# Attention and mixture of experts in one kernel: batch 0's last expert worked as a slot

## The chip, the cores and the metric

The kernel runs on one core of a Trainium2 chip. The metric is the device time in microseconds of one execution. The two kernels are timed beside each other, and an execution of each is profiled.

## What is computed

The reference is clustered attention followed by a dense mixture of experts. Attention (4 batches, 8 heads, 768 tokens, 64 values a head) lets a query see the keys of its own cluster only; its result, as x of 3072 tokens by 512, goes through all eight experts, and every expert's output is weighted by a gate that eight rounds of row and column normalisation make:

```python
x = attn(q, k, v, centroids)                  # 3072 x 512, batch after batch
P = exp(x @ w_gate - max)                     # 3072 x 8
for _ in range(8):
    P /= P.sum(1, keepdims=True) + 1e-09
    P /= P.sum(0, keepdims=True) + 1e-09
    P *= N / E
for e in range(8):
    out += P[:, e:e+1] * (maximum(x @ w1[e], 0) @ w2[e])   # 512 -> 1024 -> 512
```

## The kernel before, in words

**Stages.** The program has an attention stage, then batch 0 of the mixture of experts (lines 1422 to 1676), then batches 1 to 3 (from line 1678). Every matmul is three fp16 matmuls (high by high, high by low, low by high parts), since the reference is fp32. Scales that are powers of two (`s1`, `s2` for an expert's two matrices, `so`, `sx`) keep the parts in range. They come from the largest absolute value of a matrix.

**Seven products for eight.** Layer 1 (`layer1`, `product`, L1356) cuts 512 x 1024 weights and 512 x 768 inputs into quadrants and takes seven products of sums of quadrants, so that one step is seven products of six matmuls with 384 columns. A step treats a quarter (`f2`, 256 columns) of an expert's first matrix. The seven quadrants or sums of the weights are `A22, A11, A12, S1, S2, S3, S4`; each is stored with its high and low part in DRAM, in `w1d[i]` for step i of 32 and in `w2d[e]` for the second matrix of expert e.

**Batch 0** runs 32 steps t = 0..31, four an expert. Within a step there are seven sub-steps m = 0..6. Each emits one product of layer 1, and from m = 1 on it emits also a piece of six matmuls with 512 columns of the layer 2 of the step before (`layer2`, L1540 to L1542): layer 2 takes the eight-product form in this stage, 144 matmuls an expert. Beside these, generators are advanced a bit per sub-step: `making` turns the raw fp32 weights of step t+1 into parts (ScalarE scales and rounds, GpSimd sums and subtracts, VectorE makes the second matrix's low part), `scanning` finds the largest values of weights on ScalarE (`total`, L302) and sends them through DRAM to all partitions (`spread_powers`), `inputs` makes the inputs of batch 1, and in steps 1 to 5 the rounds of the gate normalisation ride on spare PSUM columns (`sink`). In m = 1 `store_w` (L1525) stores the finished weights for the later batches. Raw weights come in tiles of 1 MB, two loads of 512 KB each (`load_raw`, L1438), 8 tiles deep; raw tile t+7 is loaded in step t and scanned in step i-5. In the last step the four quarters of expert 0's second matrix get their sums (`second_left`, L1501), since expert 0's second matrix had been made early, and the inputs of batch 1 are loaded again (`reload_x`). At the end of an expert, `gated` (L1547) adds the gated output of six PSUM banks to `acc` by VectorE (ScalarE copies for expert 0, and `gate_first`, L1561, scales these in step 6); for expert 7 ScalarE's queue sends `acc` out. Behind the last step stands its layer 2 alone.

**Batches 1 to 3** are a list of 24 slots (batch, expert). A slot is 28 sub-steps; each emits one product of layer 1 of slot n (`layer1b`) and a quarter of one product of layer 2 of slot n-1 (`layer2b`, L1814: nine matmuls with 256 columns). Layer 2 takes seven products too, 252 matmuls an expert. What else is to be done in a slot is a table of times written out by hand (`at`, `plan_slot`, L1741): GpSimd's differences of quadrants (`minus`, L1699), the high parts `ho` on ScalarE (`high`, L1704), the low parts on VectorE (`low`, L1708), loads of the weights (`load_left`, L1712), the gates (`gate_slot`, L1736) and, during batch 1, the sums of the second matrix of experts 1 to 7 (`second_sums` and its kin). `HASTE` (L1739) replaces some of these times in the last slot. `evict` (L1781) adds a product to the four totals `C11, C12, C21, C22`. The first slot has no layer 2 beside it, and behind the last slot stands a layer 2 alone.

**Order.** After each sub-step `plan.keep_order()` pins the order of the instructions on each engine, the DMA issues on SP's queue among them, as the program emits them. A waiting instruction holds up what is behind it on its engine.

## Time and profile before

| | |
|---|---|
| time, median of 3 runs | 2287.81 us (2287.72 to 2290.61) |
| the profiled execution: time | 2289.5 us |
| the profiled execution: span from first to last instruction | 2287.7 us |
| mean granted TensorE clock | 0.998 |
| TensorE busy | 2257.7 us, 99% of the span |
| VectorE busy | 1637.3 us, 72% |
| ScalarE busy | 1113.2 us, 49% |
| GpSimd busy | 1145.9 us, 50% |
| weights' loads (TensorE), busy | 1523.3 us, 67% |
| DMA | 383.93 MB, mean 168 GB/s |

PE is the matmul side of TensorE, PEld its weight loads, DVE is VectorE, ACT ScalarE, POOL GpSimd, SP the engine whose queue issues nearly all DMAs (SPq, ACTq: instructions that issue DMAs on a queue). Times are us from the start of the span. A matmul's busy time overlaps the next one's, so the length of a stretch is read from the starts. A bracket behind a row of a timeline is the idle time of the engine ahead of the instruction and what ended it.

### The profile page before, as it was taken

The numbers are of one execution on the slowest core, as the hardware profiler recorded it, in microseconds if no ns is written. First come the engines' busy times: TensorE is split into PE (matmuls) and PEld (weight loads), VectorE is DVE, ScalarE is ACT, GpSimd is POOL, SyncE is SP. The second block draws the span as 40 slices with busy tenths as digits, with TensorE's granted clock in tenths as the row PEclk, the third lists the DMA queues.
The fourth block names the chain that finished last, engine by engine and source line by source line (L and its number), as shares of the span: only waits on it lengthen the run. The fifth ranks groups of instructions, "written<-read, shape, count | busy, mean of one in ns | idle before, by whom it ended". The sixth has DMA issues, their size and how long they took to land.

```text
span 2287.7 us, 39676 instructions
## 1 busy us (share of the span) xinstructions
PE 2257.7 (99%) x15491; PEld 1523.3 (67%) x15491; DVE 1637.3 (72%) x2691; ACT 1113.2 (49%) x2048; POOL 1145.9 (50%) x1009
## 2 busy tenths in 40 slices
PE   7999999999999999999999999999999999999998
PEld 4656665545555555567777777777777777777777
DVE  7767777648666776578888886776676666666667
ACT  5666676556666665344444443333434333333333
POOL 6676777865554555456566563333332323222233
PEclk9999999999999999999999999999999999999999
DMA  7556666446645643676666665544444554344433
GB/s 173 120 125 162 168 157 159 118 167 239 196 150 170 195 158 131 221 262 212 211 233 219 226 222 177 169 128 152 151 159 137 187 169 133 129 132 137 143 116 102
DMA packets 226828, 383.93 MB, mean 168 GB/s; under 512 B 73408, under 2 KB 154640, under 8 KB 226128
## 3 DMA queue, kind: packets, MB, share of 16 engines
q1 hardware_dynamic: 226208, 379.82, 52.6%
q8 instruction: 121, 1.98, 0.4%
q10 hardware_dynamic: 432, 1.57, 0.2%
q14 instruction: 67, 0.55, 0.1%
HBM read 272.22 MB, written 80.62 MB: 154 GB/s over the span
## 4 chain that ended last, share of the span: by engine, by line
PE 92%; DVE 3%; DMA 2%; ACT 1%; POOL 1%; issue 1%; SPq 0%; ACTq 0%; DVEq 0%; POOLq 0%
PE h_ps L1356 37%; PE pb L1814 12%; PE pc L1814 8%; PE pa L1814 8%; PE av_ps L978 5%; PE o_ps L1540 3%; PE o_ps L1542 3%; PE o_ps L1541 3%; PE max_ps L835 3%; PE exp_ps L923 3%; PE exp_ps L924 2%; PE misc_ps L636 1%; PE misc_ps L1020 1%; POOL psum L945 1%; DVE mrt L839 1%
## 5 line engine op out<-in xcount | busy, mean ns | idle before, releaser
L1356 PEld LDWEIGHTS <-wa 128*128 128x128 f16 x5376 | 525.7, 98 | 300.0 <-issue 2.1
L1814 PEld LDWEIGHTS <-ho 128*128 128x128 f16 x6048 | 591.4, 98 | 139.7 <-DVE ho L1708 2.5
L1356 PE MATMUL h_ps<-xsT,wa 128*128 128x384 f16 x3072 | 581.6, 326 | 0.3 <-DVE u L1370 0.2
L1699 POOL TENSOR_TENSOR B<-B,B 128x768 f32<-128x768 f32 x96 | 196.5, 2049 | 488.2 <-DVE ho L1708 468.0
L1356 PE MATMUL h_ps<-xsB,wa 128*128 128x384 f16 x2304 | 436.7, 326 | 0.3 <-ACT m L1379 0.3
L1708 DVE TENSOR_TENSOR ho<-B,ho 128x768 f16<-128x768 f32 x288 | 350.2, 1217 | 0.1
L1370 DVE SCALAR_TENSOR_TENSOR u<-h_ps,m 128x384 f32<-128x384 f32 x256 | 141.7, 554 | 271.1 <-PE h_ps L1356 267.0
L1854 ACT ACTIVATE B<-B 128x384 f32<-128x384 f32 x288 | 149.7, 520 | 378.8 <-DVE B L1370 375.4
L1814 PE MATMUL pb<-w2o,ho 128*128 128x256 f16 x2592 | 328.7, 273 | 0.4 <-DVE ho L1708 0.4
L1704 ACT CAST ho<-B 128x768 f16<-128x768 f32 x288 | 230.3, 825 | 11.2 <-POOL B L1699 7.8
L839 DVE TENSOR_REDUCE mrt<-max_ps 128x1 f32<-128x512 f32 (+1 forms) x288 | 190.5, 685 | 54.3 <-PE max_ps L835 52.7
L945 POOL TENSOR_TENSOR psum<-psum,pe 128x512 f32<-128x512 f32 x160 | 208.0, 1318 | 35.0 <-ACT pe L930 28.1
L1814 PE MATMUL pa<-w2o,ho 128*128 128x256 f16 x1728 | 219.2, 273 | 1.2 <-DVE ho L1708 1.2
L1814 PE MATMUL pc<-w2o,ho 128*128 128x256 f16 x1728 | 219.2, 273 | 0.2 <-DVE ho L1708 0.2
L1699 POOL TENSOR_TENSOR B<-B,T 128x768 f32<-128x768 f32 x48 | 94.6, 1973 | 230.0 <-DVE ho L1708 207.7
L930 ACT ACTIVATE pe<-exp_ps 128x512 f32<-128x512 f32 x288 | 166.9, 598 | 51.2 <-PE exp_ps L924 39.5
L1379 ACT ACTIVATE m<-h_ps 128x384 f32<-128x384 f32 x128 | 62.6, 489 | 191.0 <-PE h_ps L1356 187.2
L1852 ACT ACTIVATE B<-h_ps 128x384 f32<-128x384 f32 x96 | 47.1, 490 | 203.3 <-PE h_ps L1356 203.3
L1542 PE MATMUL o_ps<-wb,hl 128*128 128x512 f16 x384 | 145.5, 379 | 0.0
L1541 PE MATMUL o_ps<-wb,hh 128*128 128x512 f16 x384 | 145.5, 379 | 0.0
L1540 PE MATMUL o_ps<-wb,hh 128*128 128x512 f16 x384 | 145.5, 379 | 0.0
L1370 DVE SCALAR_TENSOR_TENSOR B<-h_ps,u 128x384 f32<-128x384 f32 x192 | 105.9, 552 | 48.3 <-PE h_ps L1356 48.2
(266 smaller groups left out, 3320.8 us busy)
## 6 DMA issues: line engine op xcount, KB each, us to landing
wa<-w1d SPq DMA_DIRECT2D x98, 896.0 KB
w2o<-w2d SPq DMA_DIRECT2D x168, 512.0 KB
raw<-in_moe_w SPq DMA_DIRECT2D x64, 512.0 KB
w1d<-wa SPq DMA_DIRECT2D x30, 896.0 KB
r<-in_moe_w SPq DMA_DIRECT2D x28, 512.0 KB
w2d<-w2s SPq DMA_DIRECT2D x28, 512.0 KB
w2d<-wb SPq DMA_DIRECT2D x96, 128.0 KB
scan<-in_moe_w SPq DMA_DIRECT2D x32, 256.0 KB
```

The source lines that it names most:

```text
L839: nc.vector.tensor_reduce(out=t["mr"][:, i0 : i0 + ni, ni - 1], in_=ps.rearrange("p (x c) -> p x c", x=ni), axis=AX, op=ALU.max)
L930: nc.scalar.activation(pe, ps.rearrange("p (x c) -> p x c", x=ni), AF.Exp, scale=SCALE)
L945: (nc.gpsimd if e == POOL else nc.vector).tensor_tensor(out=st[:, o : o + N0], in0=old[o], in1=part, op=ALU.add)
L1356: nc.tensor.matmul(ps[:, 0:HB], wa[:, w_, a, c, :], x[:, x_, c, :], start=(first and s_ == 0), stop=(s_ == len(steps) - 1), skip_group_che ...
L1370: nc.vector.scalar_tensor_tensor(out=t, in0=ps[:, 0:HB], scalar=KAPPA, in1=x, op0=ALU.mult, op1=ALU.add)
L1540: nc.tensor.matmul(po[i], hh[:, t, ti], wbh[:, t], start=(first and t == 0), stop=False)
L1541: nc.tensor.matmul(po[i], hh[:, t, ti], wbl[:, t], start=False, stop=False)
L1542: nc.tensor.matmul(po[i], hl[:, t, ti], wbh[:, t], start=False, stop=(last and t == 1))
L1699: nc.gpsimd.tensor_tensor(out=t, in0=d[a], in1=d[c], op=ALU.subtract)
L1704: nc.scalar.copy(t[:, 0], blocks[n, g][o])
L1708: nc.vector.tensor_tensor(out=t[:, 1], in0=blocks[n, g][o], in1=t[:, 0], op=ALU.subtract)
L1814: nc.tensor.matmul(ps[:, q], h[:, h_, f, q * P : (q + 1) * P], w[:, 2 * g + f, w_], start=(first and g == 0 and s_ == 0 and q % 2 == 0), s ...
```

## The change

Batch 0 now has 28 steps (`N1`), for experts 0 to 6. Expert 7 of batch 0 becomes the first entry of the list of slots, so there are 25 slots and its second matrix takes seven products as well. `acc` is no longer one tile but the four totals `C11, C12, C21, C22`, in which the slot goes on adding; an eviction in batch 0 becomes two operations of half the width, and batch 0's output leaves by the slots' four stores on SP. Expert 7's weights are made by a new generator, `lasting`, which starts at step 1 and is advanced in every sub-step: it loads both matrices in eight tiles of 512 KB (two deep) for the sums of absolute values, sends the largest through DRAM, then loads them once more, quarter by quarter, and makes and stores all seven quadrants or sums of both matrices. Expert 0's left-over sums (`second_left`, `step_left`) go; in their place expert 0 takes part in batch 1's `second_sums`, and expert 7 no longer does. The raw tiles are 7 instead of 8, loaded six steps ahead instead of seven. The inputs of batch 1 are reloaded in the last quarter of the first slot. In the last slot four entries of `HASTE` change or are new, and the gates are made ten sub-steps earlier.

The diff, cut to its core:

```diff
-        rawp = pool("rawp", 8, ax)
-        accp = pool("accp", 1, ax)
+        rawp = pool("rawp", 7, ax)
+        lastp = pool("lastp", 2, ax)
+    N1 = NI - NP2
+    PARTS = {"C11": (0, 0), "C22": (1, 1), "C12": (0, 1), "C21": (1, 0)}
+    accb = pool("accb", 1)
...
+        def last_first(f2):
+            raw, w = load_last(0, f2), last_tile()
...
+            yield
+            yield
+            nc.scalar.activation(raw, raw, AF.Copy, scale=s1[:, E - 1 : E])
+            yield
...
+            for o, a in quads:
+                nc.scalar.copy(y[:, 0, o], a)
+            yield
+            for o, a in quads:
+                nc.gpsimd.tensor_tensor(out=y[:, 1, o], in0=a, in1=y[:, 0, o], op=ALU.subtract)
+            yield
+            yield
+            nc.sync.dma_start(out=d[:, :, A22 : A12 + 1], in_=y)
...
+            sums(S_, A[:, 1, 0], A[:, 1, 1], A[:, 0, 0], A[:, 0, 1], nc.gpsimd)
...
+            nc.scalar.copy(y[:, 0], S_)
+            yield
+            for o in (0, 2):
+                nc.gpsimd.tensor_tensor(out=y[:, 1, o : o + 2], in0=S_[:, o : o + 2], in1=y[:, 0, o : o + 2], op=ALU.subtract)
+                yield
+            yield
+            nc.sync.dma_start(out=d[:, :, S1 : S4 + 1], in_=y)
...
+        def last_second(f2):
...
+            for o, a in quads:
+                nc.scalar.activation(y[:, o, 0], a, AF.Copy, scale=scale)
+            yield
+            for o, a in quads:
+                nc.vector.scalar_tensor_tensor(out=y[:, o, 1], in0=a, scalar=scale, in1=y[:, o, 0], op0=ALU.mult, op1=ALU.subtract)
...
+        def last_weights():
+            am = gs.tile([P, 2, NP2], F32, name="am8z", bufs=1)
+            waiting = []
+            for f2 in range(NP2):
+                for m in range(2):
+                    waiting.append((m, f2, load_last(m, f2)))
+                    yield
+                    if len(waiting) == 2:
+                        m_, f_, t = waiting.pop(0)
+                        total(am[:, m_, f_ : f_ + 1], t, t)
+                    yield
+            m_, f_, t = waiting.pop(0)
+            total(am[:, m_, f_ : f_ + 1], t, t)
+            yield
+            am2 = gs.tile([P, 2], F32, name="am2")
+            nc.vector.tensor_reduce(out=am2, in_=am, axis=AX, op=ALU.max)
+            yield from spread_powers(am2, 2, f"amw{E - 1}", lambda g: weight_use(E - 1, g, gs))
+            for f2 in range(NP2):
+                yield from last_first(f2)
+                yield from last_second(f2)
...
-                if e == 0:
-                    nc.scalar.copy(acc[:, i], ps)
-                else:
-                    gate = gates_[:, i : i + 1]
-                    nc.vector.scalar_tensor_tensor(out=acc[:, i], in0=ps, scalar=gate, in1=acc[:, i], op0=ALU.mult, op1=ALU.add)
-                if e == E - 1 and i % 2 == 1:
-                    nc.scalar.dma_start(out=out_v[0][:, i - 1 : i + 1], in_=acc[:, i - 1 : i + 1])
+                j, q_ = divmod(i, NT // 2)
+                for name, (r, j_) in PARTS.items():
+                    if j_ == j:
+                        t, s_ = acc[name][:, q_], ps[:, r * HD : (r + 1) * HD]
+                        if e == 0:
+                            nc.scalar.copy(t, s_)
+                        else:
+                            nc.vector.scalar_tensor_tensor(out=t, in0=s_, scalar=gates_[:, i : i + 1], in1=t, op0=ALU.mult, op1=ALU.add)
...
-        AHEAD = 7
+        AHEAD = 6
...
-        loads = {0: (), 1: (4, 5), 2: (6, 7, 8), 3: (9, 10)}
+        loads = {0: (), 1: (4, 5), 2: (6, 7, 8), 3: (9,)}
-        for t in range(NI):
+        for t in range(N1):
...
+            if t == 1:
+                lasting = last_weights()
...
                 if m:
                     step(before)
-                if t == NI - 1:
-                    step_left(m)
+                step(lasting)
                 if m == 1:
                     store_w(t, wt)
-                if t == NI - 1:
-                    reload_x(1, RIGHT[m])
...
-    slots = [(b, e) for b in range(1, B) for e in range(E)]
+    slots = [(0, E - 1)] + [(b, e) for b in range(1, B) for e in range(E)]
...
-    HASTE = {("T1", 1): (3, 3), ("T2", 0): (2, 4), ("T2", 1): (4, 5)}
+    HASTE = {("T1", 1): (3, 3), ("T2", 0): (1, 2), ("T2", 1): (4, 5), ("B21", 0): (5, 7), ("B21", 1): (6, 8)}
...
-        at(base - 1, gate_slot, n)
-        if e == E - 1:
+        at(base - (11 if n == NS - 1 else 1), gate_slot, n)
+        if b and e == E - 1:
...
-        if b == 1 and n:
+        if b == 1 and e < E - 1:
...
-    totals = {}
+    totals = dict(acc)
```

## Rows read from the trace of the kernel before

**Rows 1.** The page's chain that ended last: shares of the span by engine.

```profile
PE 92%; DVE 3%; DMA 2%; ACT 1%; POOL 1%; issue 1%; SPq 0%; ACTq 0%; DVEq 0%; POOLq 0%
```

**Rows 2.** Windows: us, busy us (instructions), clock, DMA share, GB/s; an expert, a slot.

```profile
735.69:794.07 58.38, 58.38 (x314) 30.53 (x313) 41.70 (x63) 38.19 (x63) 32.10 (x33) 1.00 0.57 185
1052.90:1107.70 54.80, 54.80 (x423) 41.09 (x421) 47.21 (x66) 24.14 (x39) 37.29 (x27) 1.00 0.60 182
```

**Rows 3.** Chain in time order: start us, us, what; first products of batch 0 steps.

```profile
532.06 1.95 PE h_ps L1356 x12
...
546.93 1.97 PE h_ps L1356 x12
...
722.98 1.95 PE h_ps L1356 x12
...
941.90 1.95 PE h_ps L1356 x12
```

**Rows 4.** Timeline, PE: layer 2 of the first and of the last slot begins.

```profile
993.00 1.15 PE L1814 MATMUL pa<-w2o,ho 128*128 128x256 f16 x9
...
998.16 1.14 PE L1356 MATMUL h_ps<-xsT,wa 128*128 128x384 f16 x6
...
2252.91 4.09 PE L1814 MATMUL pa<-w2o,ho 128*128 128x256 f16 x36
```

**Rows 5.** Timeline, PE: the second and third product of the first slot.

```profile
965.08 1.14 PE L1356 MATMUL h_ps<-xsT,wa 128*128 128x384 f16 x6
...
966.49 1.14 PE L1356 MATMUL h_ps<-xsB,wa 128*128 128x384 f16 x6 [0.28 <-ACT m L1379]
```

**Rows 6.** Timeline, PE: layer 2 alone, the last phase.

```profile
2256.84 2.35 PE L1814 MATMUL pc<-w2o,ho 128*128 128x256 f16 x20
...
2267.13 3.88 PE L1814 MATMUL pa<-w2o,ho 128*128 128x256 f16 x34 [1.16 <-DVE ho L1708]
...
2270.85 4.09 PE L1814 MATMUL pb<-w2o,ho 128*128 128x256 f16 x36
```

**Rows 7.** Timeline, DVE: the last phase.

```profile
2252.96 1.31 DVE L1411 TENSOR_SCALAR gates<-pr,so 128x6 f32<-128x6 f32 x1
...
2264.95 1.25 DVE L1789 SCALAR_TENSOR_TENSOR C<-pc,gates,C 128x256 f32<-128x256 f32 x3
```

**Rows 8.** Windows, columns as in rows 2: batch 0's first steps.

```profile
495.00:500.00 5.00, 5.00 (x46) 2.62 (x44) 2.67 (x7) 1.01 (x2) 0.00 (x0) 1.00 0.67 275
500.00:505.00 5.00, 5.00 (x30) 2.64 (x29) 3.99 (x10) 2.28 (x5) 0.00 (x0) 1.00 0.98 298
505.00:510.00 5.00, 5.00 (x27) 2.55 (x26) 0.98 (x3) 4.04 (x7) 3.68 (x6) 1.00 1.05 384
```

**Rows 9.** Timeline, SP's queue: step 1.

```profile
506.72 3.33 SPq L1531 DMA_DIRECT2D w2d<-wb  x3
```

**Rows 10.** Timeline, ACT: step 1.

```profile
512.99 0.53 ACT L1620 ACTIVATE hh<-c 128x384 f16<-128x384 f32 x1 [3.16 <-DVE c L1370]
```

**Rows 11.** Timeline, DVE: the end of step 3.

```profile
547.16 0.55 DVE L1370 SCALAR_TENSOR_TENSOR c<-h_ps,u 128x384 f32<-128x384 f32 x1
```

**Rows 12.** Chain in time order: an expert's largest values on their way.

```profile
701.34 5.63 DMA amw<-am
...
706.98 4.81 DMA all<-amw
```

**Rows 13.** Windows, columns as in rows 2: step 6.

```profile
576.60:591.20 14.60, 14.60 (x80) 7.64 (x79) 8.46 (x17) 12.15 (x21) 7.47 (x8) 1.00 0.41 86
```

**Rows 14.** Lines by form, 500 to 955: busy us, mean ns, idle before.

```profile
L302 ACT ACTIVATE junk<-raw 128x1024 f16<-128x1024 f32 x48 | 50.1, 1045 | 0.0
...
L1564 ACT ACTIVATE acc<-acc,gates 128x512 f32<-128x512 f32 x6 | 4.3, 712 | 0.5 <-DVE gates L1411 0.5
...
L1411 DVE TENSOR_SCALAR gates<-pr,so 128x6 f32<-128x6 f32 x7 | 1.6, 222 | 0.0
...
L1494 POOL TENSOR_TENSOR wa<-s1w,wa 128x512 f16<-128x512 f32 x60 | 78.4, 1327 | 57.0 <-ACT wa L1492 53.7 <-DMA w2d<-wb 3.3
```

More of the change, by code (lines that the diff above doesn't have):

```diff
@@ L1514, in second_left @@
+            nc.scalar.activation(y[:, :, 0], S_, AF.Copy, scale=scale)
             yield
-            nc.sync.dma_start(out=w2d[0][:, 3:7, f2], in_=y)
+            nc.vector.scalar_tensor_tensor(out=y[:, :, 1], in0=S_, scalar=scale, in1=y[:, :, 0], op0=ALU.mult, op1=ALU.subtract)
             yield
-        LEFT_AT = ((0, 3, 4, 6), (1, 5, 6, 8), (2, 7, 8, 10), (3, 9, 10, 12))
-        def step_left(now):
-            for x, times in zip(lefting, LEFT_AT):
-                if now in times:
-                    step(x)
+            yield
@@ L1673, in attn_moe_kernel @@
             rests.clear()
-            step_left(7 + m)
             step(before)
@@ L1806, in layer2b @@
                 if name not in totals:
-                    totals[name] = accp.tile([P, 3, HD], F32, name=name, bufs=2 if name == "C21" else 1)
+                    totals[name] = (accx if name == "X" or (name == "C21" and b % 2) else accb).tile([P, 3, HD], F32, name=name)
             count = 0
```

85 lines of the change are left out of this document (58 added, 27 removed).

## The prediction

> **What bounds the kernel now.** I read the page's chain of waits first: TensorE holds 92% of the chain that ended last [rows 1], so what counts is where TensorE spends columns and where it stands. The windows view then gives the price of the unit that the change moves [rows 2]: over one expert of batch 0 and over one slot TensorE is busy from end to end at full clock, while VectorE, ScalarE and GpSimd have a quarter or more of the time free. The reader is to see that both are bound by TensorE, and that only their lengths differ. The chain in time order gives the length of a step of batch 0: (941.90 - 722.98) / 15 = 14.595 us, so an expert of four steps is 58.38 us [rows 3]. The timeline of TensorE gives the slot: layer 2 of the first slot begins at 993.00 and that of the last, 23 slots later, at 2252.91, so a slot is 1259.91 / 23 = 54.78 us [rows 4].
>
> **The sum, part by part.** An execution with this span of 2287.7 us took 2289.5 us (1.8 us lie around the span), 1.7 us over the median of the runs, 2287.8. I work out a difference and set it on the median.
>
> *Expert 7 becomes a slot.* One expert of 58.38 us goes, one slot of 54.78 us comes: -3.6 us. Layer 1 is the same 28 products in both; what is saved is in layer 2, 144 matmuls of 512 columns against 252 of 256. That the narrow matmuls might cost more per column is already in the slot's measured price, so this term has one answer.
>
> *The edge between batch 0 and the slots.* Today the second product of the first slot starts at 965.08 and the third at 966.49 [rows 5], 1.41 us where two products stand 0.98 us apart: 0.43 us lost, because ScalarE's queue holds the output DMAs and expert 0's left-over weights, each waiting for VectorE. Both go away. At the end of that slot two pairs and one product take 998.16 - 993.00 = 5.16 us [rows 4] where the pace of 54.78 / 28 = 1.956 us a pair gives 4.9; the 0.26 us are VectorE's, which scales `pr` there for a batch's first expert, and the new first slot has none of that. Together -0.7 us; bounds 0 and -0.9. Against this, batch 1's inputs are now reloaded during a slot in which products stand 0.98 us apart. The first, 384 KB, can be issued about 1.2 us after its product starts and is needed 6.8 us after it; a 0.9 MB weight load stands ahead, and 1.3 MB at the 384 GB/s of [rows 8] take 3.4 us. That leaves about 2 us of cover, so 0, with 2 us as the upper bound.
>
> *The last phase.* With layer 1 over, a product takes 2256.84 - 2252.91 = 3.93 us, but the next three take 2270.85 - 2256.84 = 14.01 us: 2.2 us lost, 1.16 of it in one wait for VectorE's low half of B21 [rows 4, 6]. VectorE works there without a break. The change takes the gate operation, 1.31 us long [rows 7] where its kind takes 0.22 us on average [rows 14], out of that queue to a place ten steps earlier, puts B21's low half before the three evictions that begin at 2264.95 [rows 7], and T2's before T1's second. VectorE still has the rest of its list, so I take back what leaves the list: -1.1 us, bounds 0 and -2.2. The long gate operation stands beside GpSimd work in the same stretch. The Trainium skill, "SBUF — State Buffer", section "Who interferes with whom", has VectorE and GpSimd hold a shared port pair for a whole instruction, the other blocked; by that the 1.31 us are mostly waiting, the trace agrees, and the gain would be nearer 0.2 us than 1.1 if the next VectorE instruction merely inherits the wait.
>
> *The stream that makes expert 7's weights.* It replaces work that stood in the last steps, so its amount is nearly neutral; its place is not. Four places are priced.
>
> (a) Step 1. Eight 512 KB loads now go through the SP queue in steps 1 to 3, two tiles deep. The first stands behind raw tiles 2 to 5 and ahead of the three stores issued at 506.72 [rows 9]. Batch 0's x (1.5 MB), three stores of 128 KB and four raw tiles of 1 MB are ahead of it, 5.9 MB, of which 5 us at 275 and 5 us at 298 GB/s have moved 2.9 by 505; the other 3.0 at 384 GB/s [rows 8] last until 512.9, the load until 514.3. ScalarE reaches the sum over this tile at 512.99 - 3.16 = 509.8 [rows 10]; it waits 4.5 us, of which 3.2 were idle anyway. With the sum itself (1.05 us [rows 14] and a short read behind it) it is some 2.5 us late; that reaches TensorE only through the buffers of layer 1, as 0.7 us. The bounds are 0 and 4.5. The Trainium skill, "DMA: Bandwidth & Descriptors", section "Where 436 GB/s comes from", puts HBM at about 358 GB/s a core; the row here shows 384, so the measured rate stands, and by the page's rate the wait would be 0.6 us longer.
>
> (b) Step 3. The largest of the eight sums is taken by VectorE behind the last two sums on ScalarE. Those add over 2 us to a ScalarE already some 2 us late, so VectorE stands about 2.5 us. Its cover is thin just there, since the gates' rounds ride in steps 1 to 5: the last eviction of step 3 ends at 547.71 [rows 11] and the second product of step 4, which needs that buffer, begins one product after 546.93 [rows 3], at 547.9. I take 1.5 us; bounds 0 and 4.
>
> (c) Step 3 to 4. The maximum goes to DRAM and back: the row of another expert shows 5.63 + 4.81 = 10.4 us [rows 12], and there VectorE used it after four sub-steps. The new stream uses it three sub-steps (some 6.5 us) after issue, so VectorE stands up to 3.9 us, and the sums behind it are late. TensorE needs its next result about 2.5 us later than that queue order says: 1.4 us; bounds 0 and 3.9.
>
> (d) Step 6. ScalarE is busy 12.15 of 14.60 us there [rows 13]. Scaling the totals takes twelve half-width operations for six of 0.71 us [rows 14]: with some 0.45 us each, +1.1 us; three more operations of expert 7's second matrix fall in this step, +1.3. That fills the step; 0.6 us, bounds 0 and 2.
>
> Together +4.2 us. The rest I cost at nothing, and this hides it: one step less between a raw load and its scan (7 tiles for 8) leaves 14.6 us for 1 MB, 2.7 us of transfer; if that cover goes, ScalarE waits at the head of each step. The later loads, stores and makers fall in steps where ScalarE, VectorE and GpSimd have about 5 us free of 14.6 [rows 2]. The twice as many, half as wide evictions of an expert stand on VectorE with the same 4 us a step free. Batch 0's four stores, now on SP instead of ScalarE's queue, wait for evictions as those of later batches do, with a slot of slack behind them. Expert 0's sums take the places that expert 7's had among the slots.
>
> Sum: -3.6 - 0.7 - 1.1 + 4.2 = **-1.2 us**, so 2286.6 us. A measurement of this kernel can tell about 0.2%, 4.6 us, from no change.
>
> **The rivals.**
>
> *All of it hidden.* If the stream costs TensorE nothing, -5.4 us, 2282.4 us. For it: TensorE shows almost no stall in batch 0 although ScalarE and VectorE often run late; layer 1's two buffers and the layer 2 between them absorb some 2 us. Against it: at 547.7 the slack was 0.2 us.
>
> *The early waits reach TensorE in full (slower).* In steps 1 to 4 ScalarE waits for a load and VectorE for ScalarE and then for the DRAM round trip, in order, with every eviction of layer 1 behind them. At full length 4.5 + 4.0 + 3.9 + 0.6 = 13.0 us, so -5.4 + 13.0 = +7.6, 2295.4 us. It makes the kernel slower by more than 0.2% from 10.0 us of the 13.0 on. For it: DMA runs at its highest rate there [rows 8], and VectorE's cover in step 3 is 0.2 us. Against it: each wait must first use up what layer 1's two buffers cover.
>
> *GpSimd blocks VectorE.* In steps 4 to 22 GpSimd gets some 2.3 us more a step. If in one step of three one more VectorE operation in front of TensorE stands for a GpSimd instruction of 1.33 us [rows 14], that is 6 x 1.33 = 8.0 us: 2290.4 us with the early waits hidden, 2294.6 with them. This is what the whole-instruction lock of the Trainium skill, "SBUF — State Buffer", section "Who interferes with whom", would do. Against it: VectorE has 4.2 us a step free [rows 2], and the operations that TensorE waits for read PSUM and one tile.
>
> **How the numbers follow.** The forecast, part of the early waits reaching TensorE, gets 0.54, all hidden 0.25, the early waits in full 0.13, the block by GpSimd 0.08, half of that beyond 0.2%. So faster 0.25, same 0.54 + 0.04 = 0.58, slower 0.17. The forecast's own range is 2283.5 to 2290.5. The range given reaches down to all hidden, with a little more of the last phase's 2.2 us, 2282.0, and up to 2292.2, about where slower begins, which leaves out the 0.17 and little below.
>
> **What would show it.** Right: step starts of 14.6 us from step 7 on, the first slot beginning near 910 instead of 964, 24 slot lengths of 54.8 us, the gate operation gone from the last phase and the wait of 1.16 us there shortened; in steps 1 to 4 a ScalarE wait for the load of `lw`, a VectorE wait before `am2` and for the second DRAM tile, and TensorE's steps 2 to 5 longer than 14.87 us [rows 3] by 3 to 4 us in all. Wrong: steps 1 to 5 unchanged in length (then all hidden), or steps 8 to 22 longer than 14.6 us (then GpSimd or the later loads), or a gap at the first slot's end while an input is reloaded.

## The result, and the profile after

The changed kernel takes 2310.71 us (median of 5 runs, 2307.44 to 2313.17) where the kernel before, run beside it, takes 2289.35 us (5 runs): a ratio of 1.0089, 95% interval 1.0078 to 1.0100. The change makes the kernel slower by 0.9%; the forecast was 2286.6 us. The profiled execution, the fastest of the five, took 2307.44 us with a span of 2305.6 us, 17.9 us more than the span of before; the medians lie 21.4 us apart, and the 3.5 us between the two are in no trace. The timeline of TensorE splits the 17.9 us by the starts of the same products in both kernels:

| stretch | before | after | difference |
|---|---|---|---|
| fourth product of step 0 (at 497.50) to the first of step 6 (at 576.52) | 79.02 | 88.98 | +10.0 |
| step 6 to the first slot, without one expert of 58.38 us [rows 3] | 329.20 | 340.10 | +10.9 |
| first slot to layer 2 of the last: 24 slots, then 25 | 1288.81 | 1342.93 | +54.1 |
| the removed expert | 58.38 | | -58.4 |
| last phase [rows 4, 6] | 29.91 | 31.42 | +1.5 |

The other -0.2 us lie ahead of that fourth product and behind the last matmul of layer 2. An expert as a slot with its edge is worth 54.12 - 58.38 = -4.3 us, as forecast. The loss is 20.9 us within batch 0 and 1.5 us in the last phase, and each has its place. TensorE's timeline after, of the pieces with a wait above 1 us ahead of them in batch 0 (the bracket is the wait and what ended it):

```profile
520.91 1.14 PE L1356 MATMUL h_ps<-xsT,wa 128*128 128x384 f16 x6 [2.85 <-DVE c L1370]
538.55 0.39 PE L1622 MATMUL o_ps<-wb,hh 128*128 128x512 f16 x1 [1.64 <-ACT hh L1704]
543.11 2.08 PE L1356 MATMUL h_ps<-xsB,wa 128*128 128x384 f16 x6 [2.93 <-ACT m L1379]
...
621.79 1.14 PE L1356 MATMUL h_ps<-xsB,wa 128*128 128x384 f16 x6 [2.09 <-ACT m L1379]
694.90 1.14 PE L1356 MATMUL h_ps<-xsT,wa 128*128 128x384 f16 x6 [1.69 <-DVE c L1370]
789.33 1.14 PE L1356 MATMUL h_ps<-xsT,wa 128*128 128x384 f16 x6 [2.16 <-DVE u L1370]
800.76 1.14 PE L1356 MATMUL h_ps<-xsT,wa 128*128 128x384 f16 x6 [1.22 <-DVE c L1370]
832.12 1.14 PE L1356 MATMUL h_ps<-xsT,wa 128*128 128x384 f16 x6 [1.86 <-DVE c L1370]
```

The kernel before has no wait above 0.2 us from step 7 to the end of its batch 0. The first three stand in steps 2 and 3, right behind ScalarE's waits for the first loads of expert 7 (timeline of ScalarE, after):

```profile
517.57 1.06 ACT L302 ACTIVATE lw<-lw 128x1024 f32<-128x1024 f32 x1 [7.86 <-DMA lw<-in_moe_w]
...
536.93 1.06 ACT L302 ACTIVATE lw<-lw 128x1024 f32<-128x1024 f32 x1 [5.85 <-DMA lw<-in_moe_w]
541.53 1.06 ACT L302 ACTIVATE lw<-lw 128x1024 f32<-128x1024 f32 x1 [2.62 <-DMA lw<-in_moe_w]
```

The other five lie in steps 8, 13, 19, 20 and 22. The chain of waits after, in time order (start, us, what), shows what such transfers take, the early ones and two of the later places:

```profile
506.71 10.78 DMA lw<-in_moe_w
...
531.40 10.05 DMA lw<-in_moe_w
...
595.19 5.84 DMA amw<-am
...
616.75 1.01 POOL lw L336
...
620.21 0.02 ACT lw L1577
...
783.87 8.01 DMA w1d<-wa
...
795.68 1.57 DVE wb L1476
```

At 595 it is the largest values of another expert that go to DRAM, 5.84 us for the first way; its scales come late, so do the weights of the next step, and GpSimd, late too, does expert 7's sums (`lw`, L336) only from 616.75 on, for which ScalarE stands at 620.2 with `m1` of layer 1 behind it. At 783.87 it is the store of a finished weight tile that takes 8 us, so that its buffer comes free late. The windows after (columns as in [rows 2]): four pieces of 14.6 us, the last of them step 6 [rows 13], the 5 us behind the wait at 543.11, and the ten steps 7 to 16:

```profile
504.60:519.20 14.60, 13.46 (x72) 6.75 (x69) 5.35 (x12) 5.96 (x11) 4.88 (x6) 1.00 0.99 342
519.20:533.80 14.60, 12.89 (x72) 7.12 (x73) 12.12 (x21) 10.68 (x18) 10.29 (x10) 1.00 0.89 303
533.80:548.40 14.60, 10.04 (x46) 4.78 (x45) 7.46 (x22) 8.81 (x18) 2.99 (x4) 0.88 0.97 335
586.40:601.00 14.60, 14.60 (x80) 7.63 (x79) 9.40 (x17) 12.34 (x25) 9.55 (x10) 1.00 0.60 189
543.10:548.10 5.00, 5.00 (x20) 2.60 (x20) 2.95 (x9) 4.97 (x10) 2.76 (x4) 0.66 0.91 295
...
600.97:752.30 151.33, 146.59 (x782) 76.31 (x781) 110.48 (x191) 101.35 (x173) 108.32 (x109) 1.00 0.68 219
```

In the first three DMA is nearly full (0.99, 0.89, 0.97) at 303 to 342 GB/s. The granted clock is 0.88 in the third and 0.66 behind its longest wait; these are means over time at TensorE's two levels, 1.00 (2.4 GHz) and 0.50 (1.2 GHz). In the ten steps TensorE stands for 4.7 us of 151.3 although VectorE (110.5), ScalarE (101.4) and GpSimd (108.3) all have time free.

The last phase: the timeline of TensorE after,

```profile
2269.41 4.09 PE L1894 MATMUL pa<-w2o,ho 128*128 128x256 f16 x36
...
2278.34 1.92 PE L1894 MATMUL pc<-w2o,ho 128*128 128x256 f16 x16 [2.65 <-DVE ho L1788]
...
2289.09 3.88 PE L1894 MATMUL pb<-w2o,ho 128*128 128x256 f16 x34 [0.64 <-DVE ho L1788]
```

the place of the second row in the kernel before,

```profile
2259.37 1.92 PE L1814 MATMUL pc<-w2o,ho 128*128 128x256 f16 x16 [0.18 <-DVE ho L1708]
```

and VectorE and GpSimd in the same place after:

```profile
2270.80 2.52 DVE L1788 TENSOR_TENSOR ho<-B,ho 128x768 f16<-128x768 f32 x1
2273.24 2.56 DVE L1788 TENSOR_TENSOR ho<-T,ho 128x768 f16<-128x768 f32 x1
2275.72 2.56 DVE L1788 TENSOR_TENSOR ho<-B,ho 128x768 f16<-128x768 f32 x1
...
2268.20 4.31 POOL L1779 TENSOR_TENSOR B<-B,B 128x768 f32<-128x768 f32 x2
2272.59 2.40 POOL L1779 TENSOR_TENSOR T<-B,B 128x768 f32<-128x768 f32 x1
2274.95 2.52 POOL L1779 TENSOR_TENSOR B<-B,B 128x768 f32<-128x768 f32 x1
```

The wait of 1.16 us of [rows 6] is gone, as forecast (0.64 us stand ahead of the next product instead), but T2's low half now stands ahead of T1's second, which `pc` needs. Three low halves take 2.5 us each beside GpSimd, where one alone takes 0.94 (at 2279.39), and each ends 0.8 us after one of GpSimd's instructions has ended (2272.51, 2274.99, 2277.47). TensorE waits 2.65 us for the third where it waited 0.18.

### The profile page after: what moved, and what is told of

Its sections match the earlier page's. It is cut to its first block, busy times and chain, and to the rows that moved or that the text cites. A ratio compares the mean times of both kernels' runs of the same rounds, so it can differ in the third digit from the quotient of the medians.

```text
span 2305.6 us, 40008 instructions
## 1 busy us (share of the span) xinstructions
PE 2255.9 (98%) x15599; PEld 1532.6 (66%) x15599; DVE 1662.4 (72%) x2750; ACT 1121.8 (49%) x2078; POOL 1168.2 (51%) x1017
## 4 chain that ended last, share of the span: by engine, by line
PE 87%; DMA 4%; DVE 4%; ACT 2%; POOL 1%; issue 1%; SPq 1%; DVEq 0%; ACTq 0%; POOLq 0%
PE h_ps L1356 36%; PE pb L1894 13%; PE pc L1894 8%; PE pa L1894 8%; PE av_ps L978 4%; PE max_ps L835 3%; PE exp_ps L923 2%; PE o_ps L1622 2%; PE o_ps L1623 2%; PE o_ps L1624 2%; PE exp_ps L924 2%; DMA lw<-in_moe_w 1%; PE misc_ps L636 1%; ACT pe L930 1%; PE misc_ps L1020 1%
## 5 line engine op out<-in xcount | busy, mean ns | idle before, releaser
L1894 PEld LDWEIGHTS <-ho 128*128 128x128 f16 x6300 | 616.2, 98 | 147.0 <-DVE ho L1788 4.1
L1779 POOL TENSOR_TENSOR B<-B,B 128x768 f32<-128x768 f32 x100 | 206.5, 2066 | 514.2 <-DVE ho L1788 496.5
L1788 DVE TENSOR_TENSOR ho<-B,ho 128x768 f16<-128x768 f32 x300 | 367.5, 1226 | 0.0
L1894 PE MATMUL pb<-w2o,ho 128*128 128x256 f16 x2700 | 342.5, 273 | 0.6 <-DVE ho L1788 0.6
L1784 ACT CAST ho<-B 128x768 f16<-128x768 f32 x300 | 240.0, 825 | 11.7 <-POOL B L1779 4.0
L1894 PE MATMUL pc<-w2o,ho 128*128 128x256 f16 x1800 | 228.4, 273 | 2.7 <-DVE ho L1788 2.7
L1894 PE MATMUL pa<-w2o,ho 128*128 128x256 f16 x1800 | 228.3, 273 | 0.0
L978 PE MATMUL av_ps<-pe,vn 128*64 128x512 f32 (+1 forms) x768 | 134.2, 492 | 0.0
L1622 PE MATMUL o_ps<-wb,hh 128*128 128x512 f16 x336 | 127.5, 380 | 1.6 <-ACT hh L1704 1.6
L924 PE MATMUL exp_ps<-qX,kX 98*128 98x256 f32 (+1 forms) x384 | 126.6, 342 | 1.6 <-DMA qX<-mt 1.6
```

What stands on the lines that cost most here:

```text
L924: nc.tensor.matmul(o, t["k2"][0:98, ki], t["qa"][0:98, a:z], start=False, stop=True)
L978: nc.tensor.matmul(av[o, a:z], vn[:, i, :], heads[t]["pe", c][:, i - i0], start=(i == 0), stop=False, skip_group_check=True)
L1622: nc.tensor.matmul(po[i], hh[:, t, ti], wbh[:, t], start=(first and t == 0), stop=False)
L1779: nc.gpsimd.tensor_tensor(out=t, in0=d[a], in1=d[c], op=ALU.subtract)
L1784: nc.scalar.copy(t[:, 0], blocks[n, g][o])
L1788: nc.vector.tensor_tensor(out=t[:, 1], in0=blocks[n, g][o], in1=t[:, 0], op=ALU.subtract)
```

## The experiments

Theory A: the early loss is the loads of expert 7 in steps in which DMA is full; the later one is waits in the fixed order of each queue, where the stream uses something too soon or meets other work. Theory B: the stream is too much work beside batch 0, or GpSimd, busier, blocks VectorE. Theory C: the parts of the change outside the stream. D and E are A with places named, as the results forced them.

The end of the attention stage moves by up to 5 us from run to run (the product at 497.50 of before starts between 493.6 and 498.6), so the time of one execution misleads, and stretches of the profiled execution are compared: "early" and "later" are the first two differences of the table above, against the kernel before; "slots" and "last" are the lengths. The last column is a median for before, after, e13, e15 and e16, and one execution for the others.

| kernel | early | later | slots | last | time of one execution, or median |
|---|---|---|---|---|---|
| before | 0 | 0 | 1288.8 (24) | 29.9 | 2289.35 |
| after | 10.0 | 10.9 | 1342.9 | 31.4 | 2310.71 |
| e1 start in step 5 | 0.0 | 20.2 | 1342.9 | 32.1 | 2303.95 |
| e2 old last slot | 9.4 | 12.8 | 1342.9 | 30.0 | 2304.03 |
| e3 wide | 9.5 | 2.1 | 1342.9 | 32.0 | 2300.05 |
| e4 no scan | 0.0 | 11.2 | 1342.9 | 32.2 | 2296.30 |
| e5 start in step 7 | 0.0 | 12.4 | 1342.9 | 32.1 | 2298.32 |
| e6 four things | 0.0 | 9.9 | 1346.0 | 30.3 | 2295.46 |
| e7 no way through DRAM | 11.4 | 11.8 | 1342.9 | 31.9 | 2308.63 |
| e8 late stores | 9.2 | 8.5 | 1342.9 | 32.2 | 2306.12 |
| e9 in phase | 0.0 | 8.7 | 1348.2 | 29.9 | 2298.28 |
| e10 sooner to DRAM | 8.5 | 13.2 | 1343.4 | 32.0 | 2308.52 |
| e11 e9 and e10 | 0.0 | 11.5 | 1346.9 | 29.9 | 2301.61 |
| e12 places | 0.0 | 0.9 | 1346.1 | 30.0 | 2289.79 |
| e13 parts outside the stream, in before | 0.0 | -0.3 | 1289.4 (24) | 29.9 | 2289.72 |
| e14 no GpSimd | 9.2 | 6.6 | 1342.9 | 32.2 | 2300.29 |
| e15 three tiles | 0.0 | 3.5 | 1342.9 | 30.1 | 2288.61 |
| e16 four tiles | 0.0 | 1.7 | 1342.9 | 29.9 | 2286.57 |

e2 has the changed kernel's batch 0 as it is: 9.4 and 12.8 for 10.0 and 10.9. So a difference of 2 us in one stretch of one execution says nothing.

**The early half.** e1 and e5 move the start, e4 leaves the first loads, sums and way through DRAM out, e7 the way alone.

```diff
-            if t == 1:
+            if t == 5:      # e1;  e5: t == 7
                 lasting = last_weights()
```

> The stream begins in step 5 instead of step 1; nothing else changes. Theory A (early loads of expert 7 land late because the DMA queues are full in steps 1 to 3, and ScalarE and VectorE wait for them in order): steps 1 to 4, which lost about 10 us against the kernel before, lose at most 1 us, and the kernel comes to about 2301 us; the later 11 us stay, perhaps at other steps. Theory B (the stream's work is simply too much beside batch 0, wherever it stands): the loss moves to steps 5 to 9 and the time stays at about 2310 us. Theory C (seven raw tiles or the half-width evictions are to blame): steps 1 to 4 stay as long as they are, 2310 us.

> The stream begins in step 7, when the gates' rounds, the scaling of the totals in step 6 and the way of expert 2's largest values through DRAM are over; nothing else changes. Steps 1 to 6 should be those of the kernel before. If what expert 7's sums and its way through DRAM cost in steps 7 and 8 of the start in step 5 (about 6 us) came from meeting expert 2's way through DRAM, steps 7 to 9 lose at most 1.5 us, and the batch loses about 12 us in all, by in-order waits from step 10 on. If the amount of work decides, the loss stays near 20 us.

e4, in place of the first loads and sums:

```diff
-            for f2 in range(NP2):
-                for m in range(2):
-                    waiting.append((m, f2, load_last(m, f2)))
...
-            yield from spread_powers(am2, 2, f"amw{E - 1}", lambda g: weight_use(E - 1, g, gs))
+            for _ in range(21):
+                yield
+            for t in (s1, s2, so):
+                nc.vector.tensor_copy(out=t[:, E - 1 : E], in_=t[:, 1:2])
```

> The eight first loads of expert 7, their sums on ScalarE and the way of the largest through DRAM are left out (expert 7 takes the scales of expert 1); the rest of the stream keeps its sub-steps. Theory A: steps 1 to 4 lose at most 1 us of their 10, time about 2301 us, steps 7 to 22 unchanged. If the early loss comes from the raw tiles or from the half-width evictions instead, steps 1 to 4 stay 10 us too long.

e7, with the loads and sums kept:

```diff
-            yield from spread_powers(am2, 2, f"amw{E - 1}", lambda g: weight_use(E - 1, g, gs))
+            for _ in range(4):
+                yield
+            for t in (s1, s2, so):
+                nc.vector.tensor_copy(out=t[:, E - 1 : E], in_=t[:, 1:2])
```

> The changed kernel without the way of expert 7's largest values through DRAM and without the wait for it (it takes the scales of expert 1; four sub-steps keep the rest in place). The eight loads and sums stay. If the late loads make the early loss, steps 1 to 3 lose 8 us or more as they do, and step 4 and 5 win back at most 2 us. If the way through DRAM makes it, the early loss falls below 4 us.

In e1, e4 and e5 steps 1 to 5 are those of the kernel before to 0.01 us: the eight loads with their sums make the early loss, not the raw tiles and not the evictions. Without the way through DRAM it is as large as with it (11.4), so that way costs nothing there that these runs can tell. But e1 gains nothing in sum: its loss only moves (later 20.2), 6 us of it to steps 7 and 8. There expert 2's largest values meet the stream's loads: their first way takes 8.2 us from 580.78 on, VectorE stands 3.7 us for them, and 2.1 us more for expert 7's own at 609.98. Theory A expected the 10 us back and was wrong there; B fits e1. e5, two steps later, keeps 12.4, as expected; half of this, 6.4 us, stands in step 10, where expert 7's own largest values are under way (chain of e5: start, us, what) and VectorE stands behind them in its queue:

```profile
628.69 6.42 DMA amw<-am
635.13 4.55 DMA all<-amw
```

**The last slot.** e2 takes the old places back.

```diff
-    HASTE = {("T1", 1): (3, 3), ("T2", 0): (1, 2), ("T2", 1): (4, 5), ("B21", 0): (5, 7), ("B21", 1): (6, 8)}
+    HASTE = {("T1", 1): (3, 3), ("T2", 0): (2, 4), ("T2", 1): (4, 5)}
...
-        at(base - (11 if n == NS - 1 else 1), gate_slot, n)
+        at(base - 1, gate_slot, n)
```

> The last slot's times (HASTE) and the place of the gate operation are as before the change; the rest is the changed kernel. If the reordered last slot costs what its stretch shows (three VectorE low parts in a row, each 2.5 us beside GpSimd, ahead of the third product), the last phase shrinks from 31.4 us to the 29.9 us of the kernel before, and the time by about 1.5 us. If the longer last phase comes from something else (the totals' place, the extra slot), it stays at 31.4 us.

The last phase is 30.0 us: the reordering costs 1.4 us, and up to 2.3 in the other kernels that have it. In e1 TensorE's clock falls behind the same wait, from 0.99 to 0.50, the lower of its two levels, after 2.65 us of standing. Windows of e1, columns as in [rows 2]:

```profile
2268.80:2273.90 5.10, 2.45 (x24) 1.96 (x22) 5.10 (x4) 3.14 (x5) 4.20 (x2) 0.99 0.34 103
2273.90:2277.20 3.30, 3.30 (x16) 2.38 (x17) 3.30 (x8) 0.00 (x0) 0.00 (x0) 0.50 0.00 0
```

e9, e11, e12, e15 and e16 keep only the early gates (the old `HASTE`, the gates at base - 11): 29.9 to 30.1 us, so the gate operation's absence gains nothing. Nor do B21's earlier times: e6, which keeps them with T2's old ones, has 30.3 us; the wait of 1.16 us leaves, and waits of 0.57 and 0.63 us come. VectorE's timelines tell why the gate operation is worth nothing. e2, with it:

```profile
2267.45 1.32 DVE L1411 TENSOR_SCALAR gates<-pr,so 128x6 f32<-128x6 f32 x1
...
2269.86 3.94 DVE L1788 TENSOR_TENSOR ho<-B,ho 128x768 f16<-128x768 f32 x2
```

and e16, without it:

```profile
2250.53 5.01 DVE L1815 TENSOR_TENSOR ho<-B,ho 128x768 f16<-128x768 f32 x2
```

The two low halves behind it grow from 3.94 to 5.01 us: of the 1.32 us, 1.07 are inherited. They start earlier and end at the same time, 6.39 and 6.40 us after `pa` begins (2267.41 and 2249.14), each 0.8 us behind the end of one of GpSimd's instructions (2272.99 for the second in e2, 2254.72 in e16). That is what the whole-instruction lock of the Trainium skill, "SBUF — State Buffer", section "Who interferes with whom", would do; the prediction had named it against its own term.

**What makes the later half?** e3 only widens the stream, e8 only delays its stores, e10 only starts the other experts' ways through DRAM earlier, e14 takes GpSimd's work out of it, e13 puts the parts outside it into the kernel before.

```diff
+            yield                        # e3: two more ahead of each of the four
+            yield
             nc.scalar.activation(raw, raw, AF.Copy, scale=s1[:, E - 1 : E])
...
+            yield                        # e3: one more ahead of each first store;  e8: two ahead of every store
             nc.sync.dma_start(out=d[:, :, A22 : A12 + 1], in_=y)
...
+            yield                        # e3
+            yield
             nc.scalar.copy(y[:, 0], S_)
```

> Ten sub-steps are added to each quarter of the stream: two more between a load and its first use, two more between GpSimd's sums and their rounding, one more ahead of the first store, in both matrices. The work is the same and still starts in step 1. Theory A (what is lost in steps 7 to 22 are in-order waits of ScalarE, VectorE and SP for loads, sums and low parts that are used too soon): the 11 us lost in steps 7 to 27 fall to 5 us or less, the early 10 us stay: about 2304 us. Theory B (the amount of work, or GpSimd blocking VectorE while both run): steps 7 to 27 still lose 9 us or more, 2309 us.

> Only the stream's sixteen stores come two sub-steps later (about 4 us; on SP's queue they wait 13 to 23 us a line, over 1 us each, for low parts of GpSimd and VectorE). If SP's queue, held by these waits, makes the loss of steps 7 to 22 (late stores of finished weights and late ways through DRAM of the other experts), the loss there falls from 11 to 4 us or less. If ScalarE's waits for loads and for GpSimd's sums make it, it stays at 8 us or more. The early loss stays.

```diff
                 total(ams[e][:, m, f2 : f2 + 1], raws[idx][:, m * 1024 : (m + 1) * 1024], junkp.tile([P, 1024], F16, name="junk"))
-                yield
+                if m or f2 < NP2 - 1:
+                    yield
...
         nc.sync.dma_start(out=d, in_=am)
         yield
+        if apart:
+            yield
```

> The changed kernel, with one thing changed for experts 2 to 6: both sums of an expert's last quarter stand in one sub-step, so that its largest values start for DRAM a sub-step earlier, and a sub-step more lies between the two DMAs. Theory D: the loss of steps 7 to 22 falls from 11 to 6 us or less. If the loss is in the waits for the stream's loads and GpSimd's sums instead, it stays at 9 us or more. The early loss of 10 us stays either way.

```diff
-                nc.gpsimd.tensor_tensor(out=y[:, 1, o], in0=a, in1=y[:, 0, o], op=ALU.subtract)
+                nc.gpsimd.tensor_tensor(out=y[:, 1, o, :, 0:8], in0=a[:, :, :, 0:8], in1=y[:, 0, o, :, 0:8], op=ALU.subtract)
...
-            sums(S_, r2[:, 1, 0:HD], r2[:, 0, 0:HD], r2[:, 1, HD:DO], r2[:, 0, HD:DO], nc.gpsimd)
+            sums(S_[:, :, 0:8], r2[:, 1, 0:8], r2[:, 0, 0:8], r2[:, 1, HD : HD + 8], r2[:, 0, HD : HD + 8], nc.gpsimd)
```

> The changed kernel with GpSimd's work in the stream cut to 8 columns an operation (sums and low parts are left out; the stores of the first matrix send a tile of noughts, so they wait for nobody); loads, ScalarE's and VectorE's work and all transfers stay. If GpSimd (its lock against VectorE, ScalarE's and SP's waits for its sums and low parts) makes the loss of steps 7 to 22, it falls from 11 to 4 us or less. If loads and transfers make it, it stays at 8 us or more. The early loss of 10 us stays, since GpSimd has no part in it.

```diff
-        rawp = pool("rawp", 8, ax)
+        rawp = pool("rawp", 7, ax)
...
-                    nc.vector.scalar_tensor_tensor(out=acc[:, i], in0=ps, scalar=gate, in1=acc[:, i], op0=ALU.mult, op1=ALU.add)
+                    for h in range(2):
+                        t = acc[:, i, h * HD : (h + 1) * HD]
+                        nc.vector.scalar_tensor_tensor(out=t, in0=ps[:, h * HD : (h + 1) * HD], scalar=gate, in1=t, op0=ALU.mult, op1=ALU.add)
...
-        AHEAD = 7
+        AHEAD = 6
```

> The kernel before with three of the change's parts and nothing else: 7 raw tiles, loaded six steps ahead, and evictions (and the scaling of the totals in step 6) in two halves of 256 columns. My prediction put all three at nothing. If so, the time is that of the kernel before within 1 us. If twice as many VectorE operations at an expert's end, or the later raw loads, cost something in every expert, it is 2 us or more slower.

e13 rules out Theory C: 2289.72 us (10 runs) against 2289.21, ratio 1.000, 0.999 to 1.0009; its three parts cost nothing that this can tell (2 us). e3 answers for A: the same work, and the later loss falls from 10.9 to 2.1. It also thins the work out, to 42 sub-steps a quarter of the weights where the changed kernel has 32; e16 below, with 28, shows that this is not what helps. e8 gets 2.4 back, little more than two executions of the same code differ. e10 was a miss, and so was its theory as put: 13.2 us are no fall, and beside e2's 12.8 no rise either. Its earlier start brings the largest values back no sooner. Ahead of step 15 the first way starts 2.9 us earlier, reckoned from the step's start (720.76, after 723.11), but it now stands right behind the stores of a step's weights. On SP's queue the second DMA could be issued only 9.1 us after the first (5.2 in the changed kernel at the same place), 1.1 us later than there:

```profile
709.62 1.65 SPq L1616 DMA_DIRECT2D w2d<-wb  x3
711.37 1.61 SPq L1295 DMA_DIRECT2D amw<-am  x1
720.50 0.33 SPq L1300 DMA_DIRECT2D all<-amw  x1
```

Ahead of step 19 (780.08, after 781.49) it starts 4.8 us earlier, and the second DMA leaves 1.4 us later. In both kernels a store of the stream, `w1d<-lw`, stands ahead of this DMA on SP's queue and waits for GpSimd's low part, until 780.86 in the changed kernel. SP's queue of e10:

```profile
769.34 0.35 SPq L1295 DMA_DIRECT2D amw<-am  x1
...
780.89 0.52 SPq L1537 DMA_DIRECT2D w1d<-lw  x1
781.50 0.56 SPq L1300 DMA_DIRECT2D all<-amw  x1
```

and of the changed kernel:

```profile
775.51 0.33 SPq L1295 DMA_DIRECT2D amw<-am  x1
...
780.87 0.52 SPq L1534 DMA_DIRECT2D w1d<-lw  x1
781.48 0.56 SPq L1298 DMA_DIRECT2D all<-amw  x1
```

e14 is undecided by its own bounds: 6.6, between 4 and 8. GpSimd's work takes part in some 4 us, give or take the 2 us of above, and without it TensorE still waits for VectorE, 1.73 us at 722.70 and 2.40 us at 808.64.

**Choosing the places.** e6 combines what had helped; e9, e11 and e12 place the stream by what the trace of the one before showed; e15 and e16 bring all of it back into batch 0. These five start in step 7 and give a quarter 28 sub-steps, the length of an expert.

```diff
-        if b == 1 and e < E - 1:
+        if n == 0 or (b == 1 and e < E - 1):        # e6, e9, e11, e12: expert 7's sums in the first slot
             first = base - SLOT
...
+            for _ in range(14):                     # e9, e11: between expert 7's two DMAs
+                yield
...
+            for _ in range(8):                      # and ahead of their use
+                yield
```

> Four things together: the stream begins in step 7; its way through DRAM has two sub-steps more; two sub-steps more lie between load and use and between GpSimd's sums and their rounding, and one before a store; and the sums of expert 7's second matrix move into the first slot, where the later experts' sums are made in their own slots, which makes room for the wider distances. In the last slot B21's new times and the early gates stay, T2's go back. Theory A: batch 0 loses at most 3 us against 20.9, the last phase is 28.5 to 29 us, and the time is 2284 to 2287 us, below the kernel before. Theory B: steps 9 to 27 lose 8 us or more, 2291 us or more.

> As e6 (start in step 7, sums of expert 7's second matrix in the first slot), but each quarter of the stream now takes 28 sub-steps, just as long as an expert of four steps, and is placed so that no DMA of the stream is issued in the sub-steps in which another expert's largest values go to DRAM and back (sub-steps 3 to 7 of every fourth step); expert 7's own way through DRAM has 22 sub-steps. In the last slot only the early gates stay. Theory D (what is left of the loss is VectorE waiting for these ways through DRAM, which take 5 to 8 us instead of 2.6 to 3 where the stream's transfers meet them): batch 0 loses at most 3 us against e6's 9.9, time 2283 to 2288 us. Theory B (amount of work): still 7 us or more, 2291 us or more.

> e9 and e10 together. Theory D: no loss left in batch 0 beyond 1 us, time 2282 to 2286 us. Theory B: as e9, 2291 us or more.

e6 and e9 missed by far: 9.9 and 8.7 us are left. In e6 8.9 of them lie in steps 11, 15, 19 and 23, at the four ways of other experts through DRAM, which its transfers meet. In e9 these cost nothing or little, and other meetings show. VectorE, at expert 7's own largest values:

```profile
674.28 0.77 DVE L1602 TENSOR_SCALAR gmax<-gmax 128x2 f32<-128x2 f32 x1
675.09 1.08 DVE L1603 TENSOR_SCALAR gmax<-gmax 128x2 int32<-128x2 int32 x1
676.20 1.73 DVE L270 TENSOR_SCALAR ginv<-gmax 128x2 f32<-128x2 f32 x1
```

GpSimd at the same time:

```profile
673.87 2.27 POOL L1498 TENSOR_TENSOR wa<-s1w,wa 128x512 f16<-128x512 f32 x2 [2.11 <-ACT wa L1496]
676.10 1.80 POOL L321 TENSOR_TENSOR tx<-xqB,tx 128x768 f32<-128x768 f32 x1
```

Operations of 0.17 us in the kernel before take 0.77, 1.08 and 1.73 us here, each ending within 0.03 us of one of GpSimd's (675.03, 676.14, 677.90), and TensorE waits 1.27 and 1.24 us behind them. And where expert 7's low parts on VectorE meet the evictions of the expert before, e9 loses 1.2 to 1.4 us each time. e11 adds e10's step to e9 and loses 2.8 us more, all in steps 15, 19 and 23, those of the other experts' ways. e12 moves just these places (the diff is cut; its third place is in the first slot):

```diff
-                yield from last_first(f2)
-                yield from last_second(f2)
+                yield from last_second(f2)
+                yield from last_first(f2)
...
-            for _ in range(8):                     # from e9's way back to the use of its largest values
+            for _ in range(5):
```

> As e9 (start in step 7, sums of expert 7's second matrix in the first slot, quarters of 28 sub-steps), with three places moved that e9's trace shows late: the second matrix' low parts on VectorE go from the sub-step in which the evictions of the expert before begin to one without them; the use of expert 7's own largest values goes five sub-steps ahead, away from GpSimd's differences for batch 1's inputs; and in the first slot the four sums stand further from their rounding. Theory E (what is left, 8.7 us in batch 0 and some 2.6 us in the first slot, comes from the places where the stream's VectorE and GpSimd work meets other work): batch 0 loses 4 us or less, the first slot nothing, time 2285 to 2290 us. Theory B (the amount of work): batch 0 still loses 7 us or more.

The later loss falls to 0.9 us, with e9's work and its two tiles of 512 KB. What keeps it from gaining is the first slot, 3.2 us longer: there a product takes 0.98 us, the four sums' loads and stores crowd the transfers, and batch 1's inputs are late:

```profile
937.22 1.14 PE L1356 MATMUL h_ps<-xsB,wa 128*128 128x384 f16 x6 [2.10 <-DMA xsB<-xsd1B]
```

So e15 and e16 keep every sum in batch 0, with the two matrices' work side by side in three and four tiles of 512 KB:

```diff
-        lastp = pool("lastp", 2, ax)
+        lastp = pool("lastp", 4, ax)               # e15: 3
...
+            for i in range(29):                    # each operation of a quarter at a sub-step written out by hand
+                for time, f in todo:
+                    if time == i:
+                        f()
+                if i < 28:
+                    yield
```

> e12's idea with all of the stream back in batch 0, since e12's first slot lost 3.2 us to the four sums it had been given (the slot's transfers wait for each other there): a third tile of 512 KB lets the loads of one matrix run beside the other's work, so that a quarter with both sets of sums fits into 28 sub-steps. No DMA of it is issued in the sub-steps of another expert's way through DRAM, none of its VectorE work where the evictions stand, none of its GpSimd work at the use of the largest values. Last slot as before but for the early gates. Theory E: batch 0 loses 2.5 us or less, the first slot nothing, and the sum is -3.6 (expert to slot) - 0.8 (edge) + 2 (what is left) = about -2.5 us against the kernel before: ratio 0.998 to 1.000. Theory B (the work does not fit without loss): batch 0 loses 7 us or more, ratio 1.001 or more.

> As e15, with a fourth tile of 512 KB and the places moved that its trace shows late: ScalarE's rounding of GpSimd's sums, which in e15 stood 3.2 us for GpSimd just ahead of the sub-step in which another expert's largest values are used, now has three sub-steps and ends before it, and the load of a quarter has five sub-steps instead of three. Everything else as e15. Theory E: batch 0 loses 1.5 us or less (e15: 3.5), the first slot nothing, so about -3 us against the kernel before, ratio 0.998 to 0.9995. If 3 us of loss stay in batch 0, they belong to the work itself, ratio about 1.

e15 has 3.5 us left and takes 2288.61 us (11 runs) against 2288.70: ratio 0.9997, 0.9988 to 1.0006. e16 has 1.7 us left, 1.5 of it in step 15, one wait where an expert's largest values go to DRAM right behind those of batch 1's inputs; in the kernel before, too, the first way takes 5.6 us there [rows 12], and 6.7 here:

```profile
714.05 1.14 PE L1356 MATMUL h_ps<-xsT,wa 128*128 128x384 f16 x6 [1.68 <-DVE u L1370]
```

It takes 2286.57 us (11 runs) against 2287.66: ratio 0.9994, 0.9985 to 1.0003. From the fourth product of step 0 to the end of layer 2 its trace is 2.6 us shorter than that of before (1782.7 against 1785.3 us), which agrees with -4.3 + 1.7 and is less than the times can tell from nothing. The clearest row against B is a window of ten steps, 17 to 26, of the kernel before,

```profile
737.40:883.40 146.00, 146.00 (x782) 76.35 (x781) 102.51 (x151) 94.95 (x157) 83.97 (x82) 1.00 0.50 162
```

and the same ten of e16:

```profile
737.70:883.90 146.20, 146.20 (x782) 76.36 (x781) 115.00 (x172) 99.40 (x162) 122.95 (x117) 1.00 0.57 192
```

GpSimd is busy 122.95 us in these, against 108.32 in the changed kernel's ten steps above and 83.97 before, VectorE 115.0 against 110.5: more work than where TensorE stood for 4.7 us, and here it does not stand at all.

## Why the prediction was wrong

Two steps failed. The early waits, put at 3.6 us by (a) to (c), took 10.0, and the work that was put at nothing took 10.9.

*Expert to slot and its edge, -3.6 and -0.7.* Right: -4.3 together, in the twelve kernels whose first slot has no extra work (1342.93 us for 25 slots, in eleven of them to 0.01; 0.4 more in e10). No gap while inputs are reloaded, as costed.

*(a) Step 1, 0.7 us, bounds 0 and 4.5.* Too small: it arrives in step 2, which lost 3.0 us. The load, reckoned to land at 514.3, landed at 517.5, and ScalarE's wait was 7.86 us instead of 4.5. The rate was nearly right. A window of the changed kernel, columns as in [rows 2], shows 369 GB/s up to the landing where the sum has 384:

```profile
505.00:517.50 12.50, 12.50 (x68) 6.47 (x67) 4.92 (x10) 3.93 (x7) 4.88 (x6) 1.00 1.07 369
```

It was the bytes: 369 GB/s for 12.5 us are 4.6 MB where the sum has 3.5. Sizes counted in units of 1,048,576 bytes were set against GB/s of 10^9 (the 5.9 MB are 6.2), which is 0.3 MB. Most of the rest, by subtraction, are transfers issued behind the load, which the sum leaves out: three stores and another load of the stream were issued between 507.43 and 512.18. The 358 GB/s of the Trainium skill, "DMA: Bandwidth & Descriptors", section "Where 436 GB/s comes from", would, by the estimate in the prediction, have moved the landing by 0.6 us, of 3.2 that were missing; the measured 369 lies between the two rates.

*(b) Step 3, 1.5 us.* The place was right, the mechanism not: what stood ahead of the last sums was two more loads, 5.85 and 2.62 us late, which the prediction had not priced at all. Step 3 lost 6.7 us, and steps 1 to 5 lost 10.0 in all; part of it is the clock, which behind the wait at 543.11 was 0.66 for 5 us. The rival of the early waits in full had 13.0 us for them and was nearer.

*(c) The way through DRAM, 1.4 us.* Nothing there (e7): the loads had delayed VectorE so far that its `gmax` at 559.14 had no wait. The same way, at e5's start, cost 6.4 us: what it costs is set by what it meets.

*(d) Step 6, 0.6 us.* Nothing: 14.59 us long, ScalarE busy 12.34 of it. The stream was late, and none of the three operations of expert 7's second matrix stood in this step. In e4, where it is not late, step 6 loses 0.4 us, so the size was about right.

*"The rest I cost at nothing."* This is the step that failed most, by 10.9 us. Its reason, that the engines have about 5 us free of 14.6, is an average over a step, and the queues are in order: the largest values of every expert have four sub-steps to DRAM and back, 2.6 to 3 us of waiting for the first way where nothing meets it and 5.8 where the stream does; a rounding of sums stands for GpSimd; a store waits for low parts and holds SP (ahead of step 19). Each uses up the same cover ahead of TensorE, which the prediction itself put at some 2 us. e3, e12 and e16 show that the free time is there, once the places are chosen. That 7 tiles, the evictions and the totals cost nothing was right (e13).

*The rival of GpSimd* had 8 us and its mechanism does occur (e9, the last phase), yet more GpSimd work without a loss (e16) and 6.6 us without its work (e14) show that it is one meeting among several. How the changed kernel's 10.9 us divide among them is not settled: e8 and e14 each take a part, the parts need not add, and each was executed once.

*The last phase, -1.1 us.* +1.5. The 1.16 us wait left, as forecast, but the prediction did not ask what T2's earlier low half is put ahead of (T1's second, needed first). And it took the gate operation's 1.31 us for work, though 1.07 of it are inherited by what follows (e2 against e16); it had named that possibility and not taken it into the sum.

## What to carry to other kernels

Free time averaged over a step does not hide a stream whose operations stand in in-order queues: list for each one what is issued just ahead of and behind it, and above all what short round trip through DRAM its transfers will meet. Where the stage has a period, give the added stream the same period and put its loads, its VectorE work and its GpSimd work where the period has none of that kind; here a later start, chosen places and two more tiles took the loss in batch 0 from 20.9 to 1.7 us with the same work, and even so the kernel is not measurably faster than before. And price every load, not the first alone, by the bytes that move before it lands, those issued behind it included, and in the units of the rate.

## What the runs showed that was not expected

How long 1 KB takes to DRAM depends on the transfers it meets: 2.6 to 3 us for five of the six experts of the kernel before and 5.6 for the sixth, 5.8 beside the stream, 6.4 in e5, 8.2 in e1 and, until the second DMA could be issued, 9.1 in e10. Starting it earlier brought it back later (e10). For their length VectorE's smallest operations suffer most from GpSimd: 0.17 us became 1.73 us. And one wait of TensorE's of 2.65 us was followed by 3.3 us at a granted clock of 0.50 in e1 and by none in the changed kernel (1.00), so the last phase with this wait was 1.4 us longer than e2's in one run and 2.1 in another.
